# A long convolution beside attention: two channels in one weight load, and filter loads released by TensorE's instruction groups

## The chip, the cores and the metric

The kernel runs on one core of a Trainium2 chip. Its time is the device time of one execution in microseconds (us). Before the change the median of three executions is 828.87 us (828.64 to 829.83).

## The reference

Two independent parts are computed and put side by side, 512 output columns each, for a sequence of S = 2048.

```
A:  q, k, v = split(x @ wqkv)               # 32 heads of 16
    p = softmax(q k^T / 4)                   # per head, 2048 x 2048
    a = concat_heads(p v) @ wo
B:  k_shift = 4-tap causal convolution of k along the sequence, per channel
    kv  = k_shift * v                        # 2048 x 512
    y   = causal convolution of kv with ssm_k, 2048 taps, per channel   (by FFT in the reference)
    b   = q * (y + kv * ssm_D)
out = concat(a, b)
```

## The kernel before

**Attention.** Scores are made transposed, 128 keys by 512 queries per block: 32 heads x 4 query groups x 16 key tiles = 2048 blocks, four heads side by side on TensorE's rows (L728). Six PSUM banks (0 to 5) hold scores. In every step T, `take_banks` gives two or three of them, alternately from the lower and the upper end, and one ScalarE instruction takes the exponential of all of them into PT (L761). VectorE takes some blocks off ScalarE: one of a step's three goes through four VectorE instructions, FX, EH twice, and PTD (L803, L810, L815). TensorE multiplies the results with V (L844) into bank 6, and after a head group VectorE divides by the sums (L905 to L925).

**The convolution.** The reversed, zero-padded filters stand in DRAM (`kz_scratch`, one row of 128 + 2048 per channel). A load for one channel reads the row 128 times, each partition one element further on, so that WR holds a Toeplitz matrix of 128 x 2048 (L996, 512 KB). Four channels make a quad, `qd`; WR has 16 rows of 2048 and so four slots of a quad, and a slot is reloaded as soon as its quad is done (`load_wr`, L990; SP's queue issues the loads). The sequence is cut into 16 pieces of 128. For each quad and each of 16 lags (`conv_lags`, L1003) four matmuls run, one per channel in its own 32 columns of the array: the weights are up to 16 columns of KV (one per piece), the moving operand is 128 x 128 of WR, and the sums of all lags stay in bank 7. After four quads VectorE copies the bank to YB (L1028), after eight TensorE transposes YB back (L1039, eight transposes), and VectorE multiplies with q (L1048). There are 128 quads, 8192 matmuls.

KV, the product of k_shift and v, is made in 16 units `kv` (four groups of 128 channels, four parts each): 16 matmuls with diagonal taps DG (L468) and one VectorE product (L514). V waits for them in VST, two of whose four tiles lie in the last two rows of WR.

**What sets the order.** The program is planned while it is written out. Every engine has a list of instructions and a clock of the planner's (`Eng.op`, L131), and `advance` lets VectorE's pending work run up to a time. In each step the loop at L1241 emits the scores, the exponential, the products with V, then in `emit_bg` either a unit (projections q, k, v, `kv`, output projection `op`, `turn`) or up to LAGS = 7 lags, and at last filler matmuls that keep TensorE busy (`warm_up`, L1219). Before step N_OPEN units use bank 7; after it they need a window, in which one score bank is held back for a few steps (`take_banks`, L643, constants OPEN, REST, LEN, SLOT). The planner keeps MARGIN = 0.35 us before each exponential. `Tensor.op` (L182) counts two words for each matmul and supposes that TensorE's program comes in groups of 256 words, and that the next group lands FETCH us after the last crossing; `spare` (L204) keeps the plan from running out of instructions.

Of the kernel before, what the change touches and what calls it, by code (L numbers as in the profile page):

```python
# [9 lines left out]
U16 = mybir.dt.uint16  # L10

S = 2048
# [11 lines left out]
C = 512  # L24
NB = S // 128
PAD = 128
# [3 lines left out]
R_W = 16  # L30
# [6 lines left out]
N_OPEN = 66  # L37
# [24 lines left out]
SLOT = 16  # L62
OPEN = 80
CLOSE = 12
REST = 2
# [6 lines left out]
PLAN = 710  # L72
# [6 lines left out]
TAIL_GAP = 4  # L79
# [6 lines left out]
DMA_KB = 394  # L86
X_KB = 200
# [3 lines left out]
SOON = 0.5  # L91
NEAR = 0.2
# [4 lines left out]
CAP = 14.0  # L97
WAIT = 1.5
# [9 lines left out]
FETCH = 6.3  # L108
# [65 lines left out]
class Tensor(Eng):  # L174
# [7 lines left out]
    def op(self, fn, deps=(), **kw):  # L182
        count = Calls()
        fn(count)
        words = 2 * count.n
        t0 = self.t
        self.left = BLOCK - self.at_word % BLOCK
        h = super().op(fn, deps, **kw)
        if words >= self.left:
            part = self.left / words  # L190
            cross = self.t - (1.0 - part) * min(kw.get("run", 0.0), self.t - t0)
            stall = max(self.lands - cross, 0.0)
            if stall:
# [6 lines left out]
        return h  # L200

# [18 lines left out]
def bass_concat_heads__mha_block__ssm_conv_h3__prompt_kernel(  # L220
# [24 lines left out]
    def sb(name, shape, dt=BF16):  # L245
# [11 lines left out]
    KV = sb("KV", [128, C // 4, NB, 4])  # L257
# [34 lines left out]
           QNF[:, 0:2 * S].rearrange("p (c s) -> p c s", c=2)]  # L292
    PS = enter(nc.psum_tensor("PS", [128, 8, 512], FP32))
# [59 lines left out]
    d_outE = DmaSem(sem("d_outE"))  # L353
    d_outA = [DmaSem(sem(f"d_outA{i}")) for i in range(R_A)]
# [46 lines left out]
    h_va1 = pool.op(lambda e: e.memset(VA[:, :, :, 8 * VW:VROW].rearrange("p s k e -> p (s k) e"), 1.0))  # L401
    h_qt0 = pool.op(lambda e: e.memset(QT[:, 1:R_Q, :, :].rearrange("p r n f -> p (r n f)"), 0.0), us=(1.5, 1.6))
# [24 lines left out]
    def ready(u):  # L427
        if u[0] == "q":
            return u[1] < R_Q or 2 * (u[1] - R_Q) + 1 in qk_done
        if u[0] == "k":  # L430
            return u[1] < 2 or LAST[u[1] - 2] in qk_done
        if u[0] == "v":
            return u[1] < 2 or LAST[u[1] - 2] in pv_done
        if u[0] == "op":
            return PAIRS.index((3, u[1])) in h_otn and h_wop[0] is not None
        return KT_OF[u[1]][0] in h_kt
# [53 lines left out]
    def evac_unit(u, bank, h):  # L490
        kind = u[0]
        if kind == "q":
            p = u[1]
            last = [qk_done[2 * (p - R_Q) + i] for i in range(2)] if p >= R_Q else []
            hh = urgent(lambda e: e.tensor_scalar(QS[:, :], PS[:, bank, :], QSCALE, None, ALU.mult),
                        [h] + [h_q[2 * (p - 1) + i] if p > 1 else None for i in range(2)], us=V512)
            for par in range(2):
                for r0 in range(16 * par, 128, 32):
                    h_q[2 * p + par] = dma(pool, d_qs[p % 2][par], QT[r0:r0 + 16, p % R_Q, par, :], QS[r0:r0 + 16, :],
                                           [hh, h_qt0] + last, kb=16)  # L500
        elif kind == "k":
            _, o, sc = u
            c0 = KEYS0 if (o, sc) == (0, 0) else 0
            hh = urgent(lambda e: e.tensor_copy(KTo[:, o % 2, sc * 512 + c0:(sc + 1) * 512], PS[:, bank, c0:512]),
                        [h, qk_done[LAST[o - 2]] if o > 1 else None], us=(0.335, 0.46) if c0 else V512)
            h_k[(o, sc)] = hh
            if (o, sc) == (3, 3):
                load_wop(h)
        elif kind == "kv":
            _, c, i = u  # L510
            dst = KV[:, 32 * c:32 * c + 32, NB - 4 - 4 * i:NB - 4 * i, :]
            val = VST[c][:, NB - 4 - 4 * i:NB - 4 * i, :].rearrange("p b (k c) -> p k b c", c=4)
            src = PS[:, bank, :].rearrange("p (b k c) -> p k b c", b=4, c=4)
# [20 lines left out]
    wr_next = [0]  # L534
    h_kzw = [None]
# [449 lines left out]
    h_yb = [None]  # L985
# [3 lines left out]

    def load_wr():  # L990
        while wr_free and wr_next[0] < C // 4:
            (i, dep), qd = wr_free.pop(0), wr_next[0]
            wr_next[0] += 1
# [8 lines left out]

    def conv_lags(qd, n0, n1):  # L1003
        kk = qd % 8
        deps = [h_wr[qd], h_kvc[qd // 32]]
        r = 4 * wr_slot[qd]
        if kk % 4 == 0 and n0 == 0:
            deps.append(bank_free[BGB])

        def fn(e):  # L1010
            ins = None
            for n in range(n0, n1):
                for c in range(4):
# [6 lines left out]
        if n1 == NB:  # L1020
            wr_free.append((wr_slot[qd], h))
            load_wr()
            if kk % 4 == 3:
                half = kk // 4
# [4 lines left out]
                            [h, h_yb[0]], slack=S_C, us=V512)  # L1029
# [3 lines left out]
    def conv_turn(b, bank):  # L1033
        pbf = PS[:, bank, :].bitcast(BF16)

        def fn(e):
            ins = None
            for k in range(8):
                ins = e.transpose(pbf[:, 128 * k:128 * k + 128], YB[:, k // 4, 128 * (k % 4):128 * (k % 4) + 128],  # L1039
                                  IDN[:, :])  # L1040
            return ins
        h = pe.op(fn, [bank_free[bank], h_ybw[0], h_idn], run=0.445, kind="F")
        h_yb[0] = h
        sl = b // 8
        yv = pbf.rearrange("p (c j) -> p c j", j=32)[:, :, 0:NB].rearrange("p c j -> p j c")
        yv = bass.AP(tensor=yv.tensor, offset=pbf[:, NB - 1:NB].offset, ap=[yv.ap[0], [-1, NB], [32, CHB]])
        qv = QN[:, :, CHB * (b % 8):CHB * (b % 8) + CHB]
# [11 lines left out]
    units = [("kv", c, i) for c in range(2) for i in range(4)] + [(x, 1, i) for i in range(4) for x in "kv"]  # L1059
# [10 lines left out]
    state = {"qd": 0, "lag": 0, "turn": False, "started": False, "lags": 0.0, "left": C // 4 * NB, "t": 0.0}  # L1070
# [6 lines left out]
    def next_unit(T):  # L1077
        if T < N_OPEN:
            return early[0] if early and ready(early[0][1]) else None
        if state["turn"]:  # L1080
            return T, ("turn", state["qd"] // 8 - 1)
# [6 lines left out]
    def unit_step(T):  # L1088
# [7 lines left out]
        while not tight:  # L1096
# [23 lines left out]
            us = pe.turn("F") + (0.445 if u[0] == "turn" else 0.478 if u[0] in ("kv", "v") else 2 * MM) + SWITCH  # L1120
# [22 lines left out]
    def emit_bg(T):  # L1143
# [5 lines left out]
        if T - end[0] in tail_mm:  # L1149
            assert st["qd"] == C // 4 and not st["turn"], (T, st)  # L1150
# [3 lines left out]
        if st["qd"] == C // 4 and not st["turn"]:  # L1154
# [3 lines left out]
        if st["turn"] and st["qd"] == C // 4:  # L1158
# [11 lines left out]
        while left > 0 and st["qd"] < wr_next[0] and kv_n[st["qd"] // 32] == 4 and at(h_wr[st["qd"]]) + WAIT <= pe.t:  # L1170
            if st["turn"] and st["qd"] % 4 == 3 and st["lag"] + left >= NB:
                left = NB - 1 - st["lag"]
# [5 lines left out]
            n1 = min(n0 + left, NB)  # L1178
# [4 lines left out]
            st["lag"] = n1 % NB  # L1183
            if n1 == NB:
                st["qd"] += 1
                if st["qd"] % 4 == 0:
                    st["turn"] = st["turn"] or st["qd"] % 8 == 0
                    break

    def filler_place(limit):  # L1190
# [5 lines left out]
        if state["started"] and state["lag"]:  # L1196
            return BGB, 0, NB, 128 * (state["qd"] % 4), 1, False
# [53 lines left out]
    assert state["qd"] == C // 4 and not state["turn"] and not jobs and not part[0], (state, jobs)  # L1251
# [65 lines left out]
```

## Time and profile before

| what | value |
|---|---|
| median of 3 executions | 828.87 us |
| the profiled execution | 828.52 us, its span 826.8 us |
| granted TensorE clock, mean | 0.996 |
| exponential blocks on ScalarE / VectorE | 1771 / 277 |
| first and last exponential start | 7.9 and 818.7 us |
| first and last convolution lag | 89.5 and 804 us |
| a convolution load, issue to landing, median | 8.4 us |

In the profile PE is TensorE's matmuls, PEld its weight loads, DVE VectorE, ACT ScalarE, POOL GpSimd, SP SyncE. A row of a group reads: line, engine, operation, what is written <- what is read, shapes, count | busy us, mean ns of one | us that the engine was idle just before them, and what ended most of that. "issue" means that nothing in the profile explains the wait. A row of the windows reads: stretch, its length, busy us and count for PE, PEld, DVE, ACT and POOL, the granted clock, the busy share of the DMA engines, and GB/s. The busy tenths give 40 equal slices of the span. Instructions of one engine overlap a little, so that the distance from one start to the next is shorter than the duration shown.

### The profile page before, as it was taken

What the parts mean: (1) busy time and instruction counts of PE and PEld (TensorE: products, weight loads), DVE (VectorE), ACT (ScalarE), POOL (GpSimd) and SP (SyncE); (2) the same over time, 40 slices, a digit from 0 to 9 for tenths busy, and PEclk for the clock granted to TensorE, in tenths of its full rate; (3) what the DMA queues carried; (4) which work ended last, traced back from release to release, by engine and by line L of the source; (5) the groups of instructions that cost most, each with busy time, mean ns of one, the idle gap of its engine ahead of it and who ended that gap; (6) DMA issues with size and microseconds to landing.
All of it is one profiled execution on the core that took longest, in us unless ns stands there. A gap on an engine that the chain in (4) does not pass through costs nothing.

```text
span 826.8 us, 30549 instructions
## 1 busy us (share of the span) xinstructions
PE 762.2 (92%) x13603; PEld 324.2 (39%) x13642; DVE 794.2 (96%) x1360; ACT 807.0 (98%) x727; POOL 78.7 (10%) x155
## 2 busy tenths in 40 slices
PE   8998989999999899999899999999999999998987
PEld 3343434443333344444333344444433333333332
DVE  4999999999999899999999999999999999999985
ACT  6999999999999899999999999999999999999987
POOL 3300320010100101001011010101002002010000
PEclk9999999999999999999999999999999999999999
DMA  9998499999999999999999899999999999999922
GB/s 220 233 300 304 151 382 404 385 379 407 393 407 405 394 401 389 405 354 367 394 388 391 318 372 383 394 408 387 408 407 352 378 393 362 399 382 367 375 83 77
DMA packets 109235, 291.41 MB, mean 352 GB/s; under 512 B 37680, under 2 KB 41648, under 8 KB 108720
## 3 DMA queue, kind: packets, MB, share of 16 engines
q1 hardware_dynamic: 102256, 280.80, 90.8%
q0 software_dynamic: 5648, 8.27, 3.1%
q8 instruction: 108, 1.77, 0.9%
q10 hardware_dynamic: 1200, 0.39, 0.2%
q14 instruction: 23, 0.19, 0.1%
HBM read 276.83 MB, written 6.42 MB: 343 GB/s over the span
## 4 chain that ended last, share of the span: by engine, by line
ACT 77%; DVE 10%; PE 9%; issue 2%; DMA 1%; SPq 0%
ACT PT L761 77%; DVE EH L810 4%; PE PS L728 3%; DVE FX L803 2%; PE PS L1014 2%; PE PS L844 2%; DVE PTD L815 2%; PE PS L1219 1%; PE PS L468 1%; DMA xT<-in_A_x_dram 1%; DVE DT L905 0%; DVE YB L1028 0%; SPq L312 0%; DVE KV L514 0%; DVE OTN L925 0%
## 5 line engine op out<-in xcount | busy, mean ns | idle before, releaser
L761 ACT ACTIVATE PT<-PS 128x1024 bf16<-128x1024 f32 (+2 forms) x722 | 804.1, 1376 | 8.8 <-PE PS L728 8.3
L728 PE MATMUL PS<-QT,KTo 32*128 32x512 bf16 x2048 | 287.1, 385 | 38.7 <-ACT PT L761 14.1
L844 PE MATMUL PS<-PT,VA 128*32 128x512 bf16 x1771 | 199.7, 391 | 6.6 <-issue 3.5
L1014 PE MATMUL PS<-WR,KV 128*12 128x128 bf16 (+15 forms) x8192 | 201.6, 220 | 4.4 <-issue 4.3
L803 DVE TENSOR_SCALAR FX<-PS 128x512 f32<-128x512 f32 x277 | 187.9, 682 | 8.3 <-PE PS L728 8.0
L815 DVE SCALAR_TENSOR_TENSOR PTD<-EH,FX 128x512 uint16<-128x512 f32 x277 | 185.7, 677 | 0.0
L810 DVE SCALAR_TENSOR_TENSOR EH<-EH 128x512 f32<-128x512 f32 x277 | 185.4, 680 | 0.0
L810 DVE SCALAR_TENSOR_TENSOR EH<-FX 128x512 f32<-128x512 uint16 x277 | 184.5, 682 | 0.1
L1014 PEld LDWEIGHTS PS<-WR,KV 128*12 128x12 bf16 (+15 forms) x8192 | 140.6, 88 | 71.9 <-issue 42.5
L728 PEld LDWEIGHTS PS<-QT,KTo 32*128 32x128 bf16 x2048 | 73.3, 91 | 237.8 <-ACT PT L761 178.9
L1219 PE MATMUL PS<-IDN,ZW 128*32 128x512 bf16 (+3 forms) x498 | 132.2, 334 | 0.0
L312 POOL DMA_DIRECT2D QT<-QS x120 | 59.2, 501 | 483.7 <-DVE DR L912 133.7
L844 PEld LDWEIGHTS PS<-PT,VA 128*32 128x32 bf16 x1771 | 48.0, 93 | 114.0 <-issue 97.5
L844 PE MATMUL PS<-PTD,VA 128*32 128x512 bf16 x277 | 83.1, 383 | 0.0
L1219 PEld LDWEIGHTS PS<-IDN,ZW 128*32 128x32 bf16 x498 | 41.8, 96 | 24.1 <-issue 10.4
L905 DVE STREAM_TRANSPOSE DT<-PS 128x512 f32<-128x512 f32 x32 | 22.7, 709 | 7.3 <-PE PS L844 6.8
L1028 DVE CAST YB<-PS 128x512 bf16<-128x512 f32 x32 | 21.9, 684 | 1.4 <-PE PS L1219 1.1
L844 PEld LDWEIGHTS PS<-PTD,VA 128*32 128x32 bf16 x277 | 20.4, 95 | 1.6 <-DVE PTD L815 0.2
L955 PE MATMUL PS<-WKV,OTN 128*128 128x512 bf16 x53 | 16.9, 383 | 2.1 <-issue 1.6
L479 PE MATMUL PS<-WKV,xT 128*128 128x128 bf16 x256 | 18.1, 220 | 0.1
L456 PE MATMUL PS<-xT,WKV 128*128 128x512 bf16 (+1 forms) x52 | 15.0, 373 | 2.9 <-issue 1.1
L447 PE MATMUL PS<-xT,WQ 128*128 128x512 bf16 x45 | 14.4, 382 | 2.4 <-issue 2.1
(65 smaller groups left out, 209.2 us busy)
## 6 DMA issues: line engine op xcount, KB each, us to landing
WR<-kz_scratch SPq DMA_DIRECT2D x512, 512.0 KB, 8.4
kz_scratch<-WR SPq DMA_DIRECT2D x1, 2176.0 KB, 8.3
QN<-in_B_q_dram POOLq DMA_DIRECT2D x2, 1024.0 KB, 12.4
out_dram<-QN POOLq DMA_DIRECT2D x2, 1024.0 KB, 8.6
QT<-QS POOLq DMA_DIRECT2D x120, 16.0 KB, 5.3
out_dram<-OUTA POOLq DMA_DIRECT2D x12, 128.0 KB, 5.2
QN<-in_B_ssm_k_dram SPq DMA_DIRECT2D x1, 1024.0 KB, 8.3
OTN<-in_B_ssm_k_dram SPq DMA_DIRECT2D x1, 1024.0 KB, 9.2
```

The source lines that it names most:

```text
L312: f(outp, inp).then_inc(dsem.sem, 16)
L479: ins = e.matmul(PS[:, bank, 128 * j:128 * j + 128], lhsT=xT[:, dc, (4 * sc + j) * 128:(4 * sc + j + 1) * 128], rhs=WV[:, dc, o * 128:(o + ...
L728: ins = e.matmul(PS[:, bank, :], lhsT=KTo[32 * s:32 * s + 32, OF[n_] % 2, kt * 128:(kt + 1) * 128], rhs=QT[32 * s:32 * s + 32, n_ // 2 % R ...
L761: h_exp[T] = act.op(lambda e: e.activation(PT[:, p0:p0 + n, :].rearrange("p b f -> p (b f)"), PS[:, banks[0]:banks[0] + n, :].rearrange("p ...
L803: h_f = urgent(lambda e: e.tensor_scalar(fx, PS[:, bank, :], FIX_ADD, FIX_HI, ALU.add, ALU.min), [h, h_last.get(i - R_FX)], slack=S_FX)
L810: st["h"] = dve.op(lambda e: e.scalar_tensor_tensor(eh, src, (P1, P2)[j], src, ALU.add, ALU.mult), [st["h"], h_last.get(i - R_EH)], us=us)
L815: lambda e: e.scalar_tensor_tensor(out16, eh, P3, fx, ALU.mult, ALU.add),
L844: ins = e.matmul(dst, lhsT=w, rhs=rhs, start=(k == 0), stop=(k == KT - 1), tile_position=(0, 32 * s))
L905: h_t = urgent(lambda e: e.transpose(out=dt, in_=PS[:, PVB, :]), [h, h_mul.get(n - 1)], slack=S_T, us=(0.63, 0.751))
L1014: ins = e.matmul(PS[32 * c:32 * c + NB - n, BGB, 128 * (kk % 4):128 * (kk % 4) + 128], lhsT=KV[:, qd, n:NB, c], rhs=WR[:, r + c, 128 * (NB ...
L1028: hh = urgent(lambda e: e.tensor_copy(YB[:, half, :].rearrange("p (k i) -> p k i", k=4), src), [h, h_yb[0]], slack=S_C, us=V512)
L1219: pe.op(lambda e, s=s, k=k, rhs=rhs, bank=bank, rows=rows, c0=c0, first=first: e.matmul(PS[32 * s:32 * s + rows, bank, c0:c0 + 128 * k], l ...
```

## The change

**Two channels in a load.** The sequence is cut into 32 pieces of 64. A WR load takes 64 shifts of two channels, 64 rows apart in `kz_scratch`, on even and odd partitions: one load of 512 KB now serves two channels. KV is twice as large: on even partitions only the columns of the one channel are filled, on odd ones those of the other, the rest is zero, so that one matmul with up to 32 weight columns gives 16 pieces of both channels. There are 64 groups of eight channels (still called `qd`), each of 32 lags of four matmuls: one lag (`d = -1`) is 64 columns wide and the others 128.

**KV through a staging area.** The `kv` product is written by two VectorE instructions of 256 columns into a part of KV that isn't in use yet (STG), and four DMAs of 256 KB per 128 channels spread it to its partitions (`spread_kv`, SP's queue). GpSimd zeroes KV at the start, and a part of it again after group 15.

**Release.** WR has 12 rows, three slots. Loads of a slot go to a list; the first three are issued at once, after that four loads (one slot) are issued whenever TensorE's plan crosses into a new group of 256 words, and wait for the instruction that crossed (`on_group`, `feed_wr`).

**Turns.** After four groups (32 channels) VectorE copies the bank to YB, and TensorE turns these alone (four transposes).

**Constants.** N_OPEN 66 to 64, FETCH 6.3 to 4.2, SLOT 16 to 18, REST 2 to 4, PLAN 710 to 715, TAIL_GAP 4 to 3, SOON, NEAR, CAP and WAIT slightly; the four `kv` units of channels 128 to 255 move from before N_OPEN to after it.

```diff
-R_W = 16
+R_W = 12
-N_OPEN = 66
+N_OPEN = 64
-SLOT = 16
+SLOT = 18
-REST = 2
+REST = 4
-PLAN = 710
+PLAN = 715
-TAIL_GAP = 4
+TAIL_GAP = 3
+GATE = 4
-CAP = 14.0
-WAIT = 1.5
+CAP = 18.0
+WAIT = 1.8
-FETCH = 6.3
+FETCH = 4.2
...
             self.lands = cross + stall + FETCH
+            if kw.get("inc", True):
+                self.on_group(h)
...
-    KV = sb("KV", [128, C // 4, NB, 4])
+    KV = sb("KV", [128, C // 8, 2, 2 * NB, 4])
...
+    h_kv0[0] = pool.op(lambda e: e.memset(KV[:, :, :, :, :].rearrange("p o r u g -> p (o r u g)").bitcast(U32), 0), us=(8.8, 8.9))
     h_qt0 = pool.op(lambda e: e.memset(QT[:, 1:R_Q, :, :].rearrange("p r n f -> p (r n f)"), 0.0), us=(1.5, 1.6))
...
-            h_kvc[c] = hh = urgent(lambda e: e.tensor_tensor(dst, src, val, ALU.mult), [h, h_vn[c]], us=V512)
+            for ch in range(2):
+                dst = STG[c][:, ch, :, u0:u0 + 4, ch, :].rearrange("p o u g -> p u o g")
+                hh = (dve.op if ch else urgent)(
+                    lambda e, dst=dst, ch=ch: e.tensor_tensor(dst, src[:, :, ch], val[:, :, ch], ALU.mult),
+                    [h, h_vn[c], h_kv0[c // 3]], us=(0.335, 0.46))
+            if kv_n[c] == 3:
+                spread_kv(c, hh)
...
+    def spread_kv(c, hh):
+        for half in range(2):
+            for ch in range(2):
+                src = STG[c][64 * half:64 * half + 64, ch].rearrange("p o u k g -> p o (u k g)")
+                dst = KV[ch:128:2, 16 * c:16 * c + 16, 1 - half, :, :].rearrange("p o u g -> p o (u g)")
+                h_kvc[c] = dma(sp, d_kvc[c], dst, src, [hh, h_kvc[c - 1] if c else None] if half + ch == 0 else [], kb=256, rate=210)
...
     def load_wr():
-        while wr_free and wr_next[0] < C // 4:
+        while wr_free and wr_ahead[0] < C // 8:
...
-                src = bass.AP(tensor=kz_ap.tensor, offset=kz_ap[4 * qd + c, 0].offset, ap=[[1, 128], [1, S]])
-                h_wr[qd] = dma(sp, d_wr[i], WR[:, 4 * i + c, :], src, [h_kzw[0], dep])
+            wr_todo.extend((qd, g, dep) for g in range(4))
+            if GATE == 0 or qd < R_W // 4:
+                feed_wr(4)
+
+    def feed_wr(n, h=None):
+        for qd, g, dep in wr_todo[:n]:
+            i = wr_slot[qd]
+            row = 128 * (qd // 16) + 4 * (qd % 16) + g
+            src = bass.AP(tensor=kz_ap.tensor, offset=kz_ap[row, 0].offset, ap=[[1, 64], [64 * LKZ, 2], [1, S]])
+            h_wr[qd] = dma(sp, d_wr[i], WR[:, 4 * i + g, :], src, [h_kzw[0], dep, h], kb=512)
+            if g == 3:
+                wr_next[0] = qd + 1
+        del wr_todo[:n]
+
+    pe.on_group = lambda h: feed_wr(GATE, h)
...
+    DIST = [0, -1] + list(range(1, NLAG - 1))
...
-                for c in range(4):
-                    ins = e.matmul(PS[32 * c:32 * c + NB - n, BGB, 128 * (kk % 4):128 * (kk % 4) + 128],
-                                   lhsT=KV[:, qd, n:NB, c],
-                                   rhs=WR[:, r + c, 128 * (NB - 1 - n):128 * (NB - n)],
-                                   start=(n == 0), stop=(n == NB - 1), tile_position=(0, 32 * c))
+                d = DIST[n]
+                w = 64 if d < 0 else 128
+                for g in range(4):
+                    kv = KV[:, qd, (1 + d) % 2, (1 + d) // 2 * 2:2 * NB, g]
+                    ins = e.matmul(PS[32 * g:32 * g + 2 * ((30 - d) // 2 + 1), BGB, 128 * kk:128 * kk + w],
+                                   lhsT=kv, rhs=WR[:, r + g, S - 64 * d - 128:S - 64 * d - 128 + w],
+                                   start=(n == 0), stop=(n == NLAG - 1), tile_position=(0, 32 * g))
...
-            for k in range(8):
+            for k in range(4):
...
-    units = [("kv", c, i) for c in range(2) for i in range(4)] + [(x, 1, i) for i in range(4) for x in "kv"]
+    units = [("kv", 0, i) for i in range(4)] + [(x, 1, i) for i in range(4) for x in "kv"]
...
+    jobs += [(N_OPEN + KV1 + 4 * i, ("kv", 1, i)) for i in range(4)]
```

More of the change, by code (lines that the diff above doesn't have):

```diff
@@ L10 @@
 U16 = mybir.dt.uint16
+U32 = mybir.dt.uint32
 S = 2048
@@ L25 @@
 NB = S // 128
+NLAG = S // 64
 PAD = 128
@@ L36 @@
 BGB = 7
-N_OPEN = 66
+N_OPEN = 64
+KV1 = 1
 LAGS = 7
@@ L90 @@
 TURN = 0.2
-SOON = 0.5
-NEAR = 0.2
+SOON = 0.4
+NEAR = 0.1
 FULL = 1.6
@@ L198, in op @@
             self.lands = cross + stall + FETCH
+            if kw.get("inc", True):
+                self.on_group(h)
         self.at_word += words
         return h
+    on_group = None
     stalls = []
@@ L292, in bass_concat_heads__mha_block__ssm_conv_h3__prompt_kernel @@
            QNF[:, 0:2 * S].rearrange("p (c s) -> p c s", c=2)]
+    KVF = KV[:, :, :, :, :].rearrange("p o r u g -> p (o r u g)")
+    STG = [KVF[:, 32 * S // 16 * ((c + 1) % 4):32 * S // 16 * ((c + 1) % 4 + 1)].rearrange(
+        "p (h o u k g) -> p h o u k g", h=2, o=16, u=NB, k=2) for c in range(4)]
     PS = enter(nc.psum_tensor("PS", [128, 8, 512], FP32))
@@ L353, in bass_concat_heads__mha_block__ssm_conv_h3__prompt_kernel @@
     d_outE = DmaSem(sem("d_outE"))
+    d_kvc = [DmaSem(sem(f"d_kvc{i}")) for i in range(4)]
     d_outA = [DmaSem(sem(f"d_outA{i}")) for i in range(R_A)]
@@ L435, in ready @@
             return PAIRS.index((3, u[1])) in h_otn and h_wop[0] is not None
-        return KT_OF[u[1]][0] in h_kt
+        return KT_OF[u[1]][0] in h_kt and (u[1] < 3 or h_kv0[1] is not None)
     def pe_unit(u, bank, parts=(0, 1, 2, 3)):
@@ L510, in evac_unit @@
             _, c, i = u
-            dst = KV[:, 32 * c:32 * c + 32, NB - 4 - 4 * i:NB - 4 * i, :]
-            val = VST[c][:, NB - 4 - 4 * i:NB - 4 * i, :].rearrange("p b (k c) -> p k b c", c=4)
-            src = PS[:, bank, :].rearrange("p (b k c) -> p k b c", b=4, c=4)
-            h_kvc[c] = hh = urgent(lambda e: e.tensor_tensor(dst, src, val, ALU.mult), [h, h_vn[c]], us=V512)
+            u0 = NB - 4 - 4 * i
+            val = VST[c][:, u0:u0 + 4, :].rearrange("p b (h o g) -> p b h o g", h=2, g=4)
+            src = PS[:, bank, :].rearrange("p (b h o g) -> p b h o g", b=4, h=2, g=4)
+            for ch in range(2):
[5 more added lines that the diff above has]
+                spread_kv(c, hh)
             kv_n[c] += 1
@@ L534, in bass_concat_heads__mha_block__ssm_conv_h3__prompt_kernel @@
     wr_next = [0]
+    wr_ahead = [0]
     h_kzw = [None]
@@ L1001, in load_qn @@
                       q2[:, 256 * i:256 * i + 256].rearrange("(t p) d -> p t d", p=128), deps, kb=1860)
+    DIST = [0, -1] + list(range(1, NLAG - 1))
     def conv_lags(qd, n0, n1):
-        kk = qd % 8
-        deps = [h_wr[qd], h_kvc[qd // 32]]
+        kk = qd % 4
+        deps = [h_wr[qd], h_kvc[qd // 16]]
         r = 4 * wr_slot[qd]
-        if kk % 4 == 0 and n0 == 0:
+        if kk == 0 and n0 == 0:
             deps.append(bank_free[BGB])
@@ L1012, in fn @@
             for n in range(n0, n1):
-                for c in range(4):
-                    ins = e.matmul(PS[32 * c:32 * c + NB - n, BGB, 128 * (kk % 4):128 * (kk % 4) + 128],
-                                   lhsT=KV[:, qd, n:NB, c],
-                                   rhs=WR[:, r + c, 128 * (NB - 1 - n):128 * (NB - n)],
-                                   start=(n == 0), stop=(n == NB - 1), tile_position=(0, 32 * c))
+                d = DIST[n]
[5 more added lines that the diff above has]
+                                   start=(n == 0), stop=(n == NLAG - 1), tile_position=(0, 32 * g))
             return ins
         h = pe.op(fn, deps, run=LAG * (n1 - n0), kind="C", lat=0.4)
-        if n1 == NB:
+        if n1 == NLAG:
+            if qd == 15:
+                h_kv0[1] = pool.op(lambda e: e.memset(KVF[:, 0:2 * S].bitcast(U32), 0), [h], us=(2.2, 2.3))
             wr_free.append((wr_slot[qd], h))
             load_wr()
-            if kk % 4 == 3:
-                half = kk // 4
+            if kk == 3:
+                half = qd // 4 % 2
                 src = PS[:, BGB, :]
@@ L1028, in conv_lags @@
                 hh = urgent(lambda e: e.tensor_copy(YB[:, half, :].rearrange("p (k i) -> p k i", k=4), src),
-                            [h, h_yb[0]], slack=S_C, us=V512)
+                            [h, h_yb[half]], slack=S_C, us=V512)
                 bank_free[BGB] = h_ybw[0] = hh
@@ L1037, in fn @@
             ins = None
-            for k in range(8):
-                ins = e.transpose(pbf[:, 128 * k:128 * k + 128], YB[:, k // 4, 128 * (k % 4):128 * (k % 4) + 128],
-                                  IDN[:, :])
-            return ins
-        h = pe.op(fn, [bank_free[bank], h_ybw[0], h_idn], run=0.445, kind="F")
-        h_yb[0] = h
+            for k in range(4):
+                ins = e.transpose(pbf[:, 128 * k:128 * k + 128], YB[:, b % 2, 128 * k:128 * k + 128], IDN[:, :])
+            return ins
+        h = pe.op(fn, [bank_free[bank], h_ybw[0], h_idn], run=0.223, kind="F")
+        h_yb[b % 2] = h
         sl = b // 8
-        yv = pbf.rearrange("p (c j) -> p c j", j=32)[:, :, 0:NB].rearrange("p c j -> p j c")
-        yv = bass.AP(tensor=yv.tensor, offset=pbf[:, NB - 1:NB].offset, ap=[yv.ap[0], [-1, NB], [32, CHB]])
-        qv = QN[:, :, CHB * (b % 8):CHB * (b % 8) + CHB]
+        yv = bass.AP(tensor=pbf.tensor, offset=pbf[:, 2 * NB - 2:2 * NB - 1].offset, ap=[pbf.ap[0], [-2, NB], [1, 2], [32, 16]])
+        qv = QN.rearrange("p t (a h x) -> p t a h x", a=2, h=2)[:, :, b // 4 % 2, :, 16 * (b % 4):16 * (b % 4) + 16]
         hh = urgent(lambda e: e.tensor_tensor(qv, yv, qv, ALU.mult), [h, h_qn[sl]], slack=S_C, us=V512)
@@ L1067, in bass_concat_heads__mha_block__ssm_conv_h3__prompt_kernel @@
     jobs += [(step(9 + 7 * c) - 8, ("kv", c + 2, i)) for c in range(2) for i in range(4)]
+    jobs += [(N_OPEN + KV1 + 4 * i, ("kv", 1, i)) for i in range(4)]
     jobs += [(step(25 + 2 * qb) + 8 * t, ("op", qb, t)) for qb in range(NQB - 1) for t in range(4)]
     jobs.sort(key=lambda j: j[0])
-    state = {"qd": 0, "lag": 0, "turn": False, "started": False, "lags": 0.0, "left": C // 4 * NB, "t": 0.0}
+    state = {"qd": 0, "lag": 0, "turn": False, "started": False, "lags": 0.0, "left": C // 8 * NLAG, "t": 0.0}
     part = [None]
@@ L1080, in next_unit @@
         if state["turn"]:
-            return T, ("turn", state["qd"] // 8 - 1)
+            return T, ("turn", state["qd"] // 4 - 1)
         return next((j for j in jobs if ready(j[1])), None)
@@ L1149, in emit_bg @@
         if T - end[0] in tail_mm:
-            assert st["qd"] == C // 4 and not st["turn"], (T, st)
+            assert st["qd"] == C // 8 and not st["turn"], (T, st)
             for t, g in tail_mm[T - end[0]]:
@@ L1153, in emit_bg @@
             return
-        if st["qd"] == C // 4 and not st["turn"]:
+        if st["qd"] == C // 8 and not st["turn"]:
             if T < end[0] + min(tail_mm) and h_wop[0] is not None:
@@ L1157, in emit_bg @@
             return
-        if st["turn"] and st["qd"] == C // 4:
+        if st["turn"] and st["qd"] == C // 8:
             if T < end[0] + min(tail_mm) - 1 and at(h_ybw[0]) > pe.t - 0.2:
@@ L1169, in emit_bg @@
         left = min(LAGS, int(st["lags"]), int((room(T) - pe.turn("C") - SWITCH) / LAG), int(pe.spare() / 8))
-        while left > 0 and st["qd"] < wr_next[0] and kv_n[st["qd"] // 32] == 4 and at(h_wr[st["qd"]]) + WAIT <= pe.t:
-            if st["turn"] and st["qd"] % 4 == 3 and st["lag"] + left >= NB:
-                left = NB - 1 - st["lag"]
+        while left > 0 and st["qd"] < wr_next[0] and h_kvc[st["qd"] // 16] is not None and at(h_kvc[st["qd"] // 16]) + WAIT <= pe.t and at(h_wr[st["qd"]]) + WAIT <= pe.t:
+            if st["turn"] and st["qd"] % 4 == 3 and st["lag"] + left >= NLAG:
+                left = NLAG - 1 - st["lag"]
                 if left <= 0:
@@ L1177, in emit_bg @@
                 break
-            n1 = min(n0 + left, NB)
+            n1 = min(n0 + left, NLAG)
             left -= n1 - n0
@@ L1182, in emit_bg @@
             conv_lags(st["qd"], n0, n1)
-            st["lag"] = n1 % NB
-            if n1 == NB:
+            st["lag"] = n1 % NLAG
+            if n1 == NLAG:
                 st["qd"] += 1
                 if st["qd"] % 4 == 0:
-                    st["turn"] = st["turn"] or st["qd"] % 8 == 0
+                    st["turn"] = True
                     break
@@ L1250, in bass_concat_heads__mha_block__ssm_conv_h3__prompt_kernel @@
         T += 1
-    assert state["qd"] == C // 4 and not state["turn"] and not jobs and not part[0], (state, jobs)
+    assert state["qd"] == C // 8 and not state["turn"] and not jobs and not part[0], (state, jobs)
     assert not early_dve and not flow and not acts and not dves
```

12 lines of the change are left out of this document (7 added, 5 removed).

## The prediction

> **What bounds the kernel now.** I read the page first for the busy shares and the DMA rows. It says that two engines are full and that the DMA engines are full too:
>
> ```profile
> span 826.8 us, 30549 instructions
> ...
> PE 762.2 (92%) x13603; PEld 324.2 (39%) x13642; DVE 794.2 (96%) x1360; ACT 807.0 (98%) x727; POOL 78.7 (10%) x155
> ...
> DMA  9998499999999999999999899999999999999922
> GB/s 220 233 300 304 151 382 404 385 379 407 393 407 405 394 401 389 405 354 367 394 388 391 318 372 383 394 408 387 408 407 352 378 393 362 399 382 367 375 83 77
> ...
> q1 hardware_dynamic: 102256, 280.80, 90.8%
> ...
> q8 instruction: 108, 1.77, 0.9%
> ```
>
> ScalarE (ACT) runs the exponentials at 98%, VectorE (DVE) takes the blocks that ScalarE has no time for at 96%, and TensorE's 92% holds filler matmuls that only keep it busy. Then I asked for ScalarE's groups with shapes kept apart:
>
> ```profile
> L761 ACT ACTIVATE PT<-PS 128x1536 bf16<-128x1536 f32 x321 | 493.9, 1605 | 6.5 <-PE PS L728 6.0
> L761 ACT ACTIVATE PT<-PS 128x1024 bf16<-128x1024 f32 x398 | 429.0, 1188 | 1.0 <-PE PS L728 1.0
> ```
>
> From the start times in the trace, an exponential of three blocks follows the next by 1.330 us at best and one of two blocks by 0.903, so one block costs ScalarE 0.427. With three of four blocks, 5.3 us, the shortest possible row of exponentials is 321 x 1.330 + 398 x 0.903 + 5.3 = 791.6 us. The real one is 20.1 longer. Where those 20 us lie decides this case. Most of the idle time that can be seen is a wait for scores from TensorE (L728), so I looked at TensorE wherever it stood over 0.45 us. The longest place is near the end, in the timeline:
>
> ```profile
> 786.86 0.40 PE L844 MATMUL PS<-PT,VA 128*32 128x512 bf16 x3
> 789.23 0.40 PE L844 MATMUL PS<-PT,VA 128*32 128x512 bf16 x3 [1.98 <-issue]
> ...
> 790.21 0.61 PE L728 MATMUL PS<-QT,KTo 32*128 32x512 bf16 x3
> ...
> 791.61 0.61 PE L728 MATMUL PS<-QT,KTo 32*128 32x512 bf16 x3
> ...
> 793.53 0.39 PE L728 MATMUL PS<-QT,KTo 32*128 32x512 bf16 x3
> ```
>
> TensorE stops for 1.98 us in the middle of a group of matmuls, waiting for nothing that the profile shows ("issue"), and for 4 us after it the same matmul takes 0.61 us, not 0.39. ScalarE's timeline and the table of windows show the damage:
>
> ```profile
> 790.87 2.85 ACT L761 ACTIVATE PT<-PS 128x1536 bf16<-128x1536 f32 x2 [2.13 <-PE PS L728]
> ```
> ```profile
> 786.00:789.30 3.30, 1.22 (x22) 0.36 (x23) 3.30 (x7) 2.74 (x3) 0.00 (x0) 1.00 0.97 382
> 789.30:793.50 4.20, 4.20 (x67) 1.80 (x67) 1.70 (x3) 2.63 (x2) 0.00 (x0) 0.59 0.11 45
> ```
>
> The third last column is the granted clock: 1.00 before the stop, 0.59 after it. The stop is an instruction fetch. Queue q8 brought 108 packets, 1.77 MB, 16.4 KB each; TensorE's 27,245 recorded instructions and 335 semaphore instructions over 108 make 255 per packet. Seven stops (at 105, 223, 229, 278, 355, 649 and 787 us) stand within 30 instructions of each other in their place modulo 256, and each ends 1.3 to 1.6 us after a q8 packet has landed. Counted out over all packets, a fetch begins a median 3.2 us after TensorE passes into a new group of 256 (a tenth over 5) and takes 1.06: some 5.7 us until it can be used, while a median group lasts 7.0 us, a twentieth under 5.5. After the last convolution load, at 797 and 803 us, the fetch begins after 0.85 and 0.45 us: about 3.0 in all. So it is queueing behind the loads that makes a fetch late. ScalarE's excess over its best spacing next to these seven stops: 0.8, 0.9, 0.7, 2.5, 0.8, 0.5 and 3.2, together **9.4 us**. The other 10.7 I put down to VectorE coming late and to small change; 662 of the 719 intervals share 2.9 of it.
>
> **The change, part by part.**
>
> *Half the convolution's loads.* Now 512 loads of 512 KB, 268 MB; then 64 groups of four, 134 MB. A 4,096-byte packet takes 159 ns in the trace, so a load is 128 packets over 16 engines, 1.27 us, and a group 5.1 us. Sixty-one groups wait for a passing of TensorE; over the 715 us of convolution (89 to 804) they fill 61 x 5.1 / 715 = 43%, where the windows now show 1.0. If a passing met a load by chance, 43% of the 9.4 us would stay (4.0); if each release follows the fetch that the same passing asks for, none. Exact phase isn't to be had: the planner counts two words per matmul, without the 335 semaphore instructions, so its passings drift from the real ones by over one group across the run. I take the middle, 2.0 left: **-7.4** (ends -5.4 and -9.4). What is late next is VectorE, whose gain follows.
>
> [...]
>
> *VectorE.* L1028 (copy of four 128-column results out of PSUM) goes from 32 to 16: 16 x 0.601 (start to start) = -9.6. The product into KV becomes 32 of 256 columns for 16 of 512: the nearest 256-column row, L916, runs at 0.332, so 32 x 0.332 - 16 x 0.601 = +1.0. Net -8.6. A block on VectorE costs 4 x 0.601 = 2.40, and takes 0.427 off ScalarE; balance moves 8.6 / 2.83 = 3.0 blocks, **-1.3** (ends: none placed, 0; 3.6 blocks, -1.5).
>
> *TensorE.* Four times 32 lags over 64 groups is 8,192 matmuls, as before, of 128 columns (64 in one lag). Their spacing, 0.0555 us per four, is the same from 1 to 16 weight columns; the change has up to 32. Weight loads of 32 columns are in L844: four begin within 10 ns of each other and take 93 ns, against 84 to 92 for 1 to 16 columns. Ends: nothing, or 93 - 56 = 37 ns per lag if a load no longer hides, 0.26 us in a burst of seven against the 0.35 us that the planner keeps before each exponential, up to 10 us of ScalarE. I take nothing, since the L468 row sustains a 128-column load per 56 ns. The 64 transposes fewer (L1039, 56 ns each, 3.6 us) lie under the filler matmuls (132 us).
>
> [...]
>
> *GpSimd.* Zeroing KV is 8,192 words: by its QT row (2,048 elements, 1.79 us) 7.2 us, or 14.3 if bytes count. It has an idle stretch of 9.9 us from 5.4 (waiting for SHK); the rest delays only the DG mask by some 5 us, which a unit needs from step 35, beyond 40 us. Hidden. A second zeroing of 2 us comes in mid-run, when GpSimd (10% busy) has only QT copies, due 24 steps ahead.
>
> *Spreading KV.* 16 DMAs of 1,024 packets of 256 bytes; such a packet takes 18 ns, so 1.15 us each. Channels 0 to 127 are spread some 20 steps before the convolution starts, the others far ahead. On SP's queue they stand before loads that have slack of a ring slot (11 us). Hidden; if not, up to 5 us once.
>
> *Moved units and constants.* Four products go from the opening into windows, in which a 3-bank exponential becomes a 2-bank one: 0.016 us per lost bank (three pairs cost 2.709, two triples 2.660). Twenty either way are 0.3; one more block for VectorE at the end is -0.4. I put them at nothing, ends -0.7 and +0.7.
>
> Sum against the profiled execution, 828.52 (span 826.8 and 1.7 around it): 828.5 - 7.4 - 1.3 = 819.8. The median is 0.35 above that execution: **820.2**.
>
> **The rivals.**
>
> *Fetches are no cheaper (828.9 - 1.3 = 827.6, within 0.2%).* If what delays a fetch is any load in flight and not the queue's length, the stops stay and 1.3 is left. For: a new group arrives at each passing. Against: 3.2 us with loads, 0.45 to 0.85 without. [...]
>
> *More stops than before (836, slower).* The planner's fetch time goes from 6.3 to 4.2 us, so it may pack TensorE closer. If groups of 256 shorten by 1 us, a quarter lie under 5.4; if the fetch stays at 5.7, half of those, 13, stop at 9.4 / 7 = 1.34: 828.9 - 1.3 - 9.4 + 17.4 = 835.6. It decides from about eight stops more than now. For: the uncounted semaphores. Against: a mean fetch must get faster with half the bytes.
>
> *Weight loads show (about 829).* Worked out above, up to 10 us; the L844 rows speak against it.
>
> *More than the stops (814).* With 8.6 us freed, VectorE is late less often: all 9.4, 1.3 and 4 of the other 10.7, 828.9 - 14.7.
>
> **How the numbers follow.** Forecast (817 to 824.5) 0.58; more than the stops 0.13; no cheaper fetch 0.11; more stops 0.13; weight loads 0.05, half of it faster. Range 811 to 829: all but the slower case and part of the last. A kernel like this can be told from no change at about 0.2%, 1.7 us: faster 0.74, same 0.12, slower 0.14.
>
> **What would show it.** Right: WR rows x256 and DMA tenths near 5; q8 packets beginning 1 to 2 us after a passing; at most three stops over 0.7 us with an "issue"; ScalarE's wait for L728 down from 8.3 to about 3; L1028 x16; 279 to 281 blocks on VectorE. Wrong: stops as many as now, windows with a clock near 0.6, a lag's spacing above 0.06, or TensorE waiting for WR.

## The result and the profile after

The changed kernel takes 822.09 us (median; 820.86 to 823.32), the kernel before in the same series 828.89: a ratio of 0.9922 (95% interval 0.9901 to 0.9942), that is, 0.8% faster. Run once more in another series it gave 821.20 against 827.07, 0.994 (0.9922 to 0.9958). The profiled execution took 821.08, its span 819.3, 7.5 us less than before.

The page after, the lines that answer to those of before:

```profile
span 819.3 us, 30354 instructions
...
PE 771.0 (94%) x13602; PEld 327.2 (40%) x13602; DVE 793.1 (97%) x1372; ACT 804.6 (98%) x731; POOL 87.4 (11%) x157
...
DMA  9994279568876666666886656666563636630010
GB/s 231 226 296 110 77 222 332 188 237 253 319 259 250 229 223 223 238 217 244 235 249 199 221 209 207 233 214 214 208 207 130 214 112 232 208 117 14 2 53 26
...
q1 hardware_dynamic: 82032, 150.76, 55.7%
...
q8 instruction: 107, 1.75, 0.8%
```

The DMA engines fell from full to about six tenths, and q1, which carries the loads, from 281 to 151 MB. ScalarE and VectorE are as full as before, over a shorter span. ScalarE's groups by shape, and all that ScalarE waited for:

```profile
L789 ACT ACTIVATE PT<-PS 128x1536 bf16<-128x1536 f32 x310 | 480.0, 1620 | 2.2 <-PE PS L756 2.2
L789 ACT ACTIVATE PT<-PS 128x1024 bf16<-128x1024 f32 x413 | 443.6, 1195 | 0.3
```
```profile
ACT KTo L630 <- PE PS L617: 3.3, 1, 3.3
ACT PT L789 <- PE PS L756: 3.2, 5, 1.1
ACT QT L1001 <- PE PS L983: 3.0, 1, 3.0
```

The second row of waits was 8.3 us in 12 places. By start times, the shortest row of exponentials is now 310 x 1.330 + 413 x 0.903 + 5.3 = 790.5 us (791.6 before), and the real one is 13.5 us longer (20.1 before). These two differences, 1.1 and 6.6, are 7.7 together and account for the 7.5 us. Five stops by an instruction fetch are left (124, 173, 287, 294 and 466 us). The longest of them, in TensorE's timeline:

```profile
293.29 0.39 PE L756 MATMUL PS<-QT,KTo 32*128 32x512 bf16 x3
294.99 0.40 PE L872 MATMUL PS<-PT,VA 128*32 128x512 bf16 x3 [1.30 <-issue]
...
295.87 0.39 PE L756 MATMUL PS<-QT,KTo 32*128 32x512 bf16 x3
```

It has the form of those of before, but is shorter, and the matmul after it keeps its 0.39 us. The windows around it show the clock at 1.00 (third last column):

```profile
290.00:293.60 3.60, 3.45 (x78) 1.51 (x68) 3.54 (x8) 3.60 (x4) 0.00 (x0) 1.00 0.88 340
293.60:297.00 3.40, 2.10 (x59) 1.19 (x56) 3.40 (x7) 2.59 (x3) 0.00 (x0) 1.00 0.07 23
```

### The profile page after: what moved, and what is told of

Read it like the earlier page. It is cut to its first block, busy times and chain, and to the rows that moved or that the text cites. A ratio compares the mean times of both kernels' runs of the same rounds, so it can differ in the third digit from the quotient of the medians.

```text
span 819.3 us, 30354 instructions
## 1 busy us (share of the span) xinstructions
PE 771.0 (94%) x13602; PEld 327.2 (40%) x13602; DVE 793.1 (97%) x1372; ACT 804.6 (98%) x731; POOL 87.4 (11%) x157
## 4 chain that ended last, share of the span: by engine, by line
ACT 95%; PE 3%; issue 1%; DMA 1%; DVE 0%
ACT PT L789 95%; PE PS L756 1%; PE PS L1061 1%; PE PS L872 1%; DMA xT<-in_A_x_dram 1%; PE PS L461 0%; PE PS L617 0%; DVE DT L933 0%; ACT QT L1001 0%; PE PS L1266 0%; PE PS L983 0%; DVE QT L627 0%; DVE DTN L944 0%; PE PS L1087 0%; DVE OTN L953 0%
## 5 line engine op out<-in xcount | busy, mean ns | idle before, releaser
L1061 PE MATMUL PS<-WR,KV 128*30 128x128 bf16 (+8 forms) x8192 | 216.0, 220 | 2.9 <-issue 2.9
L843 DVE SCALAR_TENSOR_TENSOR PTD<-EH,FX 128x512 uint16<-128x512 f32 x280 | 188.1, 678 | 0.2
L838 DVE SCALAR_TENSOR_TENSOR EH<-FX 128x512 f32<-128x512 uint16 x280 | 187.0, 683 | 0.1
L1061 PEld LDWEIGHTS PS<-WR,KV 128*28 128x28 bf16 (+7 forms) x8192 | 149.8, 95 | 81.0 <-issue 49.5
L872 PE MATMUL PS<-PTD,VA 128*32 128x512 bf16 x280 | 85.8, 383 | 0.6 <-DVE PTD L843 0.6
L983 PE MATMUL PS<-WKV,OTN 128*128 128x512 bf16 x64 | 19.7, 385 | 0.3 <-DVE OTN L953 0.3
L470 PE MATMUL PS<-xT,WKV 128*128 128x512 bf16 (+1 forms) x64 | 17.9, 377 | 0.6 <-DVE KTo L518 0.5
L461 PE MATMUL PS<-xT,WQ 128*128 128x512 bf16 x60 | 17.5, 384 | 0.0
L493 PEld LDWEIGHTS PS<-WKV,xT 128*128 128x128 bf16 x256 | 14.4, 98 | 7.0 <-issue 5.4
```

The source lines that it names most:

```text
L493: ins = e.matmul(PS[:, bank, 128 * j:128 * j + 128], lhsT=xT[:, dc, (4 * sc + j) * 128:(4 * sc + j + 1) * 128], rhs=WV[:, dc, o * 128:(o + ...
L838: st["h"] = dve.op(lambda e: e.scalar_tensor_tensor(eh, src, (P1, P2)[j], src, ALU.add, ALU.mult), [st["h"], h_last.get(i - R_EH)], us=us)
L843: lambda e: e.scalar_tensor_tensor(out16, eh, P3, fx, ALU.mult, ALU.add),
L872: ins = e.matmul(dst, lhsT=w, rhs=rhs, start=(k == 0), stop=(k == KT - 1), tile_position=(0, 32 * s))
L983: ins = e.matmul(PS[:, bank, :], lhsT=OTN[:, PAIRS.index((o, qb)), t * 128:(t + 1) * 128], rhs=WO[:, o, :], start=(o == 0), stop=(o == 3))
L1061: ins = e.matmul(PS[32 * g:32 * g + 2 * ((30 - d) // 2 + 1), BGB, 128 * kk:128 * kk + w], lhsT=kv, rhs=WR[:, r + g, S - 64 * d - 128:S - 6 ...
```

## The experiments

The theory is that of the prediction: the queue of loads delays TensorE's instruction fetch, the stops that follow hold up ScalarE, and half the bytes take most of them away; freed time of VectorE adds a little. The rivals: the new plan misses the stops by itself; the release behind the fetch does it, not the bytes; the plan misplaces the passings. Each run was timed against the kernel before on its own chip (829.04 us for the first four, 827.03 for the next four, 827.07 for the last four). The "delay" is the median time from a passing, counted out over TensorE's recorded instructions, to the start of the next q8 packet; a stop is counted when TensorE stood over 0.45 us at the place of a passing and resumed 1.2 to 1.8 us after such a packet had landed. Both come from the one profiled execution of each run. Some instruction records are missing from the traces (53 of the output projection's 64 matmuls stand in that of the kernel before and in that of after_half_more_loads), so a delay is uncertain by a few tenths (the prediction had 3.2 for the kernel before, the table has 3.4).

| run | mean GB/s | delay, us | stops | us | ratio to before (95%) |
|---|---|---|---|---|---|
| before | 352 | 3.4 | 7 | 828.89 | |
| changed | 197 | 1.8 | 5 | 822.09 | 0.9922 (0.9901 to 0.9942) |
| before_half_loads | 197 | 2.0 | 1 | 821.97 | 0.9921 (0.9897 to 0.9946) |
| after_half_more_loads | 275 | 3.4 | 18 | 833.26 | 1.0071 (1.0046 to 1.0095) |
| after_no_wait | 196 | 2.3 | 7 | 823.86 | 0.9965 (0.9939 to 0.9991) |
| after_plan_716 | 196 | 2.1 | 7 | 823.89 | 0.9955 (0.9931 to 0.998) |
| after_exact_words | 196 | 1.7 | 1 | 823.21 | 0.9953 (0.9935 to 0.9971) |
| before_exact_words | 354 | 2.9 | 4 | 826.24 | 1.0003 (0.9985 to 1.0021) |

**before_half_loads: the bytes alone.** Every instruction of the kernel before stays in its place; only the loads shrink.

```diff
-                src = bass.AP(tensor=kz_ap.tensor, offset=kz_ap[4 * qd + c, 0].offset, ap=[[1, 128], [1, S]])
-                h_wr[qd] = dma(sp, d_wr[i], WR[:, 4 * i + c, :], src, [h_kzw[0], dep])
+                n = S if qd < R_W // 4 else S // 2
+                src = bass.AP(tensor=kz_ap.tensor, offset=kz_ap[4 * qd + c, 0].offset, ap=[[1, 128], [1, n]])
+                h_wr[qd] = dma(sp, d_wr[i], WR[:, 4 * i + c, 0:n], src, [h_kzw[0], dep])
```

> The kernel before with every load after the first four quads cut to half its bytes (columns 0 to 1023; the other half of the slot keeps old data, so the output is not the convolution). Same instructions in the same order on all engines, half the bytes in flight. If the queue of loads ahead of the instruction fetch makes the stops: a fetch begins about 1.8 us after the passing instead of 3.4, at most two of the seven stops are left, and the time falls by 5 to 9 us, to 820 to 824. If the stops belong to the plan and the bytes are innocent: seven stops, 828.9 within 1 us.

Measured: 821.97 us, the time of the changed kernel, with the same plan, the same count of blocks on VectorE and one stop by a fetch. From its page and its waits:

```profile
span 819.9 us, 30549 instructions
...
DMA  9998375777665777667679277666776657676612
...
q1 hardware_dynamic: 102256, 150.77, 63.2%
```
```profile
ACT PT L761 <- PE PS L728: 2.7, 5, 1.0
```

30,549 instructions and 102,256 packets on q1, as before, with about half the bytes; the stop at 787 us, which cost 3.2, is gone. So fewer bytes are enough for the whole gain. Neither the new plan nor the release is needed for it: here a load is still issued as soon as its slot is free. Between medians this run gains 7.1 us and the changed kernel 6.8, so VectorE's relief doesn't show in the time beside it.

**after_half_more_loads and after_double_loads: the bytes put back.** SP issues further copies behind each group of four, in a plan that is otherwise the changed kernel's: two in the one run, as shown, and all four in the other.

```diff
+    def load_more(src):
+        i, more[0] = more[0] % 8, more[0] + 1
+        ds, v = d_more[i], d_more[i].n
+        ds.add()
+        sp.ops.append(([(ds.sem, v)] if v else [], lambda e: e.dma_start(more_ap[128 * i:128 * i + 128, :], src).then_inc(ds.sem, 16), None))
...
+        for src in srcs[:2]:
+            load_more(src)
```

> The changed kernel, and behind each group of four loads SP issues four more copies of the same 512 KB rows from DRAM to a DRAM scratch that nothing reads: about twice the bytes, the same instructions and order on TensorE, VectorE and ScalarE. If the queue of loads makes the stops: fetches begin near 3.4 us after the passing again, the five short stops become ten or more, and the time rises by 4 to 9 us, to 826 to 831. If the new plan avoids the stops by itself: 822 within 1 us.

Measured: 938.64 us (1.1336). This says little about fetches: with the engines full again, a load comes 11.6 us after its issue (6.2 in the changed kernel), and TensorE waits for the data itself.

```profile
PE PS L1075 <- DMA WR<-kz_scratch: 66.7, 28, 5.5
```

> The changed kernel, plan as it is, with two extra 512 KB copies (DRAM to a DRAM scratch that nothing reads) behind each group of four loads: half more bytes. The run with four was spoilt by TensorE's waits for WR (67 us); these should stay under 5 us here. If the queue of loads delays fetches: delay over 2.3 us, eight stops or more, 824 to 830. If not: 822 within 1 us.

Measured: delay 3.4 us, 18 stops, 833.26 us, somewhat more than expected. TensorE's row of lags now shows the fetch as the larger part and the data as the smaller:

```profile
L1075 PE MATMUL PS<-WR,KV 128*28 128x128 bf16 (+8 forms) x8192 | 219.7, 220 | 14.6 <-issue 11.4 <-DMA WR<-kz_scratch 3.0
```

In the changed kernel the same row stands at 2.9 "issue". From both sides, then, the stops go with the bytes: 7 to 1 with half of them in the old plan, 5 to 18 with half more in the new one.

**after_no_gate, after_no_wait, after_no_gate_fetch_6_3: the release.**

```diff
-GATE = 4
+GATE = 0
```

> The changed kernel with GATE = 0: the four loads of a slot are issued as soon as the slot is free, not with TensorE's passing into a new group. If half the bytes is all that counts: 822 within 1.5 us (the plan shifts a little), and about as many stops. If the release behind the fetch is what makes it early: fetches begin at 2.5 us or later, ten stops or more, 825 to 829.

Measured: 834.08 us (1.0057; 1.0033 to 1.0081), delay 2.7, six stops, ScalarE's wait for scores 14.5 us. That was worse than either theory had it, but GATE = 0 also makes a new plan. So the plan was kept, and only the wait left out of the loads:

```diff
-            h_wr[qd] = dma(sp, d_wr[i], WR[:, 4 * i + g, :], src, [h_kzw[0], dep, h], kb=512)
+            h_wr[qd] = dma(sp, d_wr[i], WR[:, 4 * i + g, :], src, [h_kzw[0], dep], kb=512, after=h)
...
+        eng.t = max(eng.t, at(after) + 0.06)
```

> The changed kernel with its plan and all instructions as they are, and only the loads' wait for TensorE's passing left out: SP issues a load once its slot is free. If the release behind the fetch is what keeps fetches early: the delay of a fetch rises from a median 1.8 us towards 2.7, eight stops or more, and 826 to 833. If the run without the gate lost because its plan came out worse: 822 within 1 us.

Measured: 823.86 us, 0.9965 of before, between the two expectations; delay 2.3, seven stops. Against the changed kernel's two ratios (0.9922 and 0.994) the gate is worth 0.25 to 0.43%, 2 to 3.6 us, but the intervals overlap: its sign is likely, not shown, and its size not settled. The gate hardly keeps loads away from fetches. Call a load in flight when over 30 of its packets begin between 0.3 us before a passing and 0.7 us after it: of 100 passings between 92 and 790 us, 57 meet a load without the wait and 52 with it.

> The changed kernel without the gate (GATE = 0) and with the planner's old fetch time, FETCH = 6.3. If the gate is needed because the plan counts on 4.2 us: the stops go down to three or fewer and the time from 834 to 822 within 2 us. If loads issued at once are bad by themselves: 830 or more.

Measured: 828.83 us (1.0007), four stops. Both expectations miss: by the ratios, the longer fetch time in the plan brought back about 4 us of the 10 to 11 that GATE = 0 had cost, not all. One stop of 2.4 us at 164 us is left in it, and one wait of 6.9 us of VectorE for a QT copy. What made these two plans bad beyond their stops stays open.

**after_plan_716: the control.** `PLAN = 716` for 715.

> A control: the changed kernel with PLAN 716 for 715, which shifts due times by a step and so reshuffles the plan without touching a mechanism. If the differences between plans are small change: 822 within 1.5 us. If the plan's luck is as large as what is looked for: 3 us or more away from 822, and then a run whose plan was made anew says little by its time alone.

Measured: 823.89 us, 0.9955, seven stops, 279 blocks on VectorE; that is between the two expectations. Shifting due times by a step costs 0.15 to 0.33%, 1 to 3 us. A run whose plan is made anew can't show less than that by its time; the runs with an unchanged plan (before_half_loads, after_no_wait, both runs with more loads) carry the verdict.

**after_16_more_copies: VectorE's relief undone.**

```diff
+                hh = dve.op(lambda e: e.tensor_copy(YB[:, half, :].rearrange("p (k i) -> p k i", k=4), src), [hh], us=V512)
```

> The changed kernel with each of the 16 copies of the convolution's bank to YB made twice, that is, VectorE's relief undone. If VectorE's free time turns into blocks: 277 blocks on VectorE instead of 280 and 1.3 us more, 823.4, beside what a shifted plan does (about 1.5 us either way). If VectorE has time to spare: 280 blocks and 822.

Measured: 833.42 us (1.0081; 1.0047 to 1.0115). The count of blocks came out as expected, 277:

```profile
L831 DVE TENSOR_SCALAR FX<-PS 128x512 f32<-128x512 f32 x277 | 187.9, 685 | 6.2 <-PE PS L756 5.7
```

But the time rose by 11 us and not by 1.3. The profile shows two other costs. TensorE's transposes wait for the second copy,

```profile
PE PS L1088 <- DVE YB L1078: 8.5, 9, 1.9
```

and there are six stops by a fetch in the new plan. What share of the 11 us each has isn't shown. The balance of blocks is confirmed; the time of this run isn't that of the balance.

**after_exact_words, before_exact_words, after_exact_words_by_threes: the planner's count.** The planner now counts the semaphore instructions too.

```diff
-        words = 2 * count.n
         t0 = self.t
...
         h = super().op(fn, deps, **kw)
+        words = 2 * count.n + max(len(self.ops[-1][0]) - 1, 0)
```

> The changed kernel with the planner counting TensorE's separate semaphore instructions too (one for each wait beyond the first of an instruction), so that its passings agree with the real ones to the end and each release stands right behind the fetch. If the drift of the passings leaves the stops: a fetch begins about 1 us after the passing, at most one stop by a fetch, and 2 to 4 us less than the changed kernel, 818 to 820, but for a new plan's luck of 2 us. If not: as many stops as now and 822 to 824.

Measured: one stop by a fetch instead of five, as expected, and yet 823.21 us. The profiled execution, at 826.92 us the slowest of the twelve, lost time at one place: at 124 us TensorE waits for a load,

```profile
126.39 0.57 PE L1061 MATMUL PS<-WR,KV 128*32 128x128 bf16 x16 [2.26 <-DMA WR<-kz_scratch]
126.89 0.61 PE L756 MATMUL PS<-QT,KTo 32*128 32x512 bf16 x3
```

and ScalarE loses 5.0 us there; the matmul takes 0.61 again, and the granted clock from 124 to 130 us was 0.67. How much of that the median execution pays isn't shown. SP's issues around that place:

```profile
96.91 18.20 SPq L323 DMA_DIRECT2D WR<-kz_scratch  x8
115.20 13.05 SPq L323 DMA_DIRECT2D KV<-KV  x4
128.29 7.60 SPq L323 DMA_DIRECT2D WR<-kz_scratch  x8
```

The load that TensorE waited for is the last of the first row, issued at 114.5. So the spreading of KV (second row) stands behind it, and the loads that stand behind the spreading begin at 128.3, after the wait. The four loads of this group were released at 112.6 us, in the changed kernel at 107.1; they landed 7.7 us later than there (126.35 for 118.69). The later release is 5.5 us of that; what made the rest is open.

> The kernel before with the same correction of the count and all its loads. If it is the wrong place of the passings in the plan that makes its seven stops: at most three, and 821 to 824. If it is the loads in flight: six stops or more, and 827 to 831.

Measured: 826.24 us (1.0003). The profile has four stops, none over 0.62 us, and ScalarE's wait for scores is down from 8.3 to 3.8 us, but with 275 blocks on VectorE and two more on ScalarE. Neither expectation holds. The profiled execution took 824.60 us, in a run that goes from 823.06 to 831.12, so its short stops may not stand for the median. Whether misplaced passings have a part in the stops of the kernel before isn't settled; correcting them alone doesn't give the gain.

> The changed kernel with the exact count and three loads released at a passing instead of four: 3.8 us of loads at a time instead of 5.1. If the length of a burst still delays fetches: 1 to 2 us less than with fours. If the release behind the fetch already suffices: the same within the plan's luck of 2 us.

Measured: 823.04 us (0.9955; 0.9938 to 0.9972), one stop, delay 1.1. The same as with fours within the plan's luck. No version here beats the changed kernel.

> The changed kernel itself once more, beside the other runs of this chip: 0.992 of before, within 0.003.

Measured: 821.20 us, 0.994, five stops again, four of them at the same places.

## Why the prediction was right, point by point

- **The fetch stops** (predicted -7.4, between -5.4 and -9.4). They went from seven to five, and ScalarE's excess beside them from 9.4 to 3.5 us: -5.9. The mechanism is shown by before_half_loads (seven stops to one, delay 3.4 to 2.0 us) and after_half_more_loads (five to 18, 1.8 to 3.4). The size was off by 1.5: what is left lies near the "by chance" end (4.0), not in the middle between it and "never". The releases didn't keep loads clear of the fetches: a load was in flight at 52 of 100 passings (before_half_loads 77 of 100, the kernel before 96 of 99). At those 52 the fetch began after a median 2.8 us, at the other 48 after 1.0. Three stops at most were forecast over 0.7 us, and there were three (0.83, 1.10 and 1.28) and two shorter ones. The delay fell from 3.4 to 1.8, inside the 1 to 2 that were named. The forecast scaled the 9.4 as a whole. In fact two stops with a lowered clock behind them made 5.7 of it, and these are gone; the other five made 3.7, and five like them are left (see the last section).
- **VectorE** (-1.3, three blocks). 280 blocks instead of 277, L1028's row from 32 to 16 copies, the 256-column product at 415 ns for a row that gave 415. The shortest row of exponentials fell by 1.1: three blocks are 1.3, and the shift from triples to pairs gave 0.2 back. No run shows this 1.1 as time by itself: after_16_more_copies confirms the blocks alone.
- **TensorE** (nothing). A lag's spacing stays at 0.055 to 0.057 us up to 32 weight columns, though a load of 32 columns takes a median 107 ns against 84 for two. The four loads of a lag begin within a median 10 ns of each other, at 32 columns as at two. One behind the other they would take 4 x 107 = 428 ns; at 0.055 to 0.057 us a lag they overlap.
- **GpSimd** (hidden). Zeroing KV took 6.9 us (7.2 by the row taken), and GpSimd still waited 2.4 us for SHK.
- **Spreading KV** (hidden, or 5 us once). Hidden in the changed kernel, where TensorE waited 0.2 us for WR. But the cost was taken from the wrong row: the packets are quick (18 ns), while SP needs 4 to 13 us to issue four such DMAs (0.6 to 6.4 each), and loads behind them are issued that much later: in the changed kernel the four that begin at 113.92 us hold the queue for 9.62, and the next load begins at 123.58. No run shows that this cost time; the 5.0 us lost in after_exact_words came with a load issued ahead of the spreading.
- **Constants and windows** (nothing). What is left of ScalarE's excess, 10.7 before, is 10.0: small change, as put.
- **The sum**: -7.4 - 1.3 = -8.7 predicted; -5.9 - 1.1 - 0.7 = -7.7 by these parts, -7.5 in the span, -6.8 between medians. The term that was too large is the first. Part of the closeness may be luck: another plan of the same kernel moves the time by 1 to 3 us.
- **The rivals.** "Fetches are no cheaper" fell. By count most passings show no stop: of some 108, seven do before and five after. But the seven cost 9.4 us, and with half the bytes most of that went. "More stops than before" didn't come, but isn't far off: half as many bytes again bring 18 stops and 833 us. "Weight loads show" fell by the lag's spacing. "More than the stops" didn't come: of the other 10.7, 10.0 are left.

## What to carry to other kernels

Where an engine has thousands of short instructions and the DMA engines are full, as in the kernel before, look for idle time by "issue" that ends soon after a packet of the instruction queue has landed (1.3 to 1.6 us at the seven stops). There fewer bytes may shorten the kernel although no engine waits for the data itself: half the loads' bytes alone took off 7.1 us here (before_half_loads). Before trusting a time, see how much a change of plan alone moves it (1 to 3 us here), and test a cause in a copy of the program in which nothing else moves. A DMA of many small pieces should be priced by the issuing queue too, not by its packets alone (18 ns a packet here, but 1.5 us of the queue in the median for 1,024 of them), though here that was hidden.

## What had not been expected of the hardware

- After a stop of 2.0 us in the kernel before the granted clock was 0.59 in the next 4 us, and after one of 1.6 us 0.67; in the changed kernel it stayed at 1.00 after stops of 1.1 and 1.3 us. ScalarE lost 3.2 us by the stop of 2.0 and 2.5 by that of 1.6, but 1.3 and 1.0 by those of 1.1 and 1.3. So two stops made 5.7 of the 9.4 us before; the other five cost 3.7 together, about as much as the five that are left (3.5). Length alone doesn't decide: in before_half_loads the clock fell to 0.50 after a stop of 1.24 us at 105 us, and in after_half_more_loads it stayed at 1.00 after one of 1.39 us at 225 us (the mean of that execution is 1.0). The windows behind the stop of 1.6 us (before) and behind that of 1.24 us (before_half_loads):

```profile
282.00:286.00 4.00, 4.00 (x81) 1.81 (x73) 3.16 (x6) 2.87 (x3) 0.00 (x0) 0.67 1.03 406
```
```profile
107.60:111.00 3.40, 3.40 (x71) 1.73 (x67) 3.40 (x6) 3.24 (x3) 0.00 (x0) 0.50 0.79 249
```

- Copies within SBUF, the on-chip memory, of 1,024 pieces of 256 bytes hold SP's queue for 1.5 us in the median and up to 6.4; a load of 128 pieces of 4,096 bytes holds it for 0.61 in the changed kernel and 0.43 in the kernel before.
